# Linear attention and a gated MLP on one core: banks of two classic products, half the copies of m on VectorE, one of eight products by 1/den on Pool

## Chip, cores, metric

One core of one Trainium2 chip runs the whole kernel. The metric is the device time of one execution in microseconds. The kernel before took 230.46 us (median of three runs, 230.44 to 230.59). TensorE is written PE, VectorE DVE, ScalarE ACT and GpSimd POOL, as in the profile. The calls ran on different chips (1, 2, 1 and, for the last kernel, 15; that of the first result is not on record), so times are compared within a call and ratios between calls.

## The reference

2048 tokens, width 512, 32 heads of 16, gated width 896, all in bf16:

```python
def _A_ref(x, wqkv, wo):                       # linear attention
    q, k, v = ...                              # x @ wqkv, 32 heads
    phi = lambda t: jnp.where(t > 0, t + 1, jnp.exp(t)) + 1e-06
    pq, pk = phi(q), phi(k)
    kv = einsum('bhsd,bhse->bhde', pk, v);  z = einsum('bhsd->bhd', pk)
    num = einsum('bhqd,bhde->bhqe', pq, kv)
    den = einsum('bhqd,bhd->bhq', pq, z)[..., None] + 1e-06
    return heads_joined(num / den) @ wo
def _B_ref(x, w_in, w_sp, b_sp, w_out):        # gated MLP
    z = gelu(x @ w_in);  z1 = z[..., :Fh];  z2 = layernorm(z[..., Fh:])
    g = einsum('ts,bsf->btf', w_sp, z2) + b_sp[None, :, None]
    return (z1 * g) @ w_out
h  = x + _A_ref(layernorm(x), A_wqkv, A_wo)
h2 = h + _B_ref(layernorm(h), B_w_in, B_w_sp, B_b_sp, B_w_out)
```

## The kernel before

The program is a list of operations with their dependencies. A stored permutation, ORDER, gives the queue of every engine. An operation that is recorded through a helper carries the helper's line, so L402 is any product, L421 any ACT instruction and L555 any normalization. The parts that matter here (cuts marked with `# ...`):

```python
    for c in range(KD):                            # m = block-diagonal(kv) @ wo, KD = 4
        b = CB[1 - c % 2]
        matmuls(bank(b), [(kvm[:, c, :], wo[:, c, :])])
        act(m[:, c, :], bank(b), ACT.Copy, GW)     # four copies PSUM -> SBUF on ACT
    # ...
    for tg in range(NG):                           # four groups of 512 tokens
        # den on PE, 1/den by Ln and Exp on ACT, spread by 4 DMAs into r16, then
        for t in range(first, tg + 1):
            for c in range(0, KD, 2):
                q, r = pqT[:, c:c + 2, t * GW:(t + 1) * GW], r16[t // 2][:, c:c + 2, t % 2, :]
                dve(lambda v, q=q, r=r: v.tensor_tensor(q, q, r, ALU.mult), [q, r], [q], 2 * GW, acc=2)
    # ...
    for n in range(NT):                            # 16 tiles of 128 tokens
        b = AB[n % 3]
        matmuls(bank(b), [(pqT[:, c, n * P:(n + 1) * P], m[:, c, :]) for c in range(KD)])
        dve(... scalar_tensor_tensor(h[:, n, :], bank(b), 1.0, x[:, n, :], ..., accum_out=s[:, 0:1]) ...)
        act(sh_t[n % 2], h[:, n, :], ACT.Square, D, ...)
        # per pair of tiles: mean and variance in five small steps on POOL, the last of them
        pool(lambda p: p.tensor_tensor(r, ve, expo..., ALU.pow), ...)            # rs, L546
        # then, per tile of the pair:
        norm("DVE", hn, h[:, i, :], ...)           # DVE tensor_scalar bf16 -> bf16, L555
        dma_t(hnT[:, :, i * P:(i + 1) * P], hn, f"ht{i}")                         # transposing DMA
    # ...
    for q in (0, 1):                               # ungated half of z, most of it by Strassen
        for tg in (2 * q, 2 * q + 1):
            classic(KF - 1, tg, 6)                 # the odd block as plain products, in bank 6
        # ... strassen(k, q, ZB[...], ...): banks 4 to 7
```

Names used below: a bank is a part of PSUM, numbered 0 to 7, to which PE writes a product. m is the block-diagonal kv times wo; h is x plus the attention's output, hn its normalization and hnT the transpose of that, made by DMA. The products of hnT with the half of w_in that becomes z2 (L807 and L810, win2 in the prediction) make, for one tile of tokens, a gated unit. wsp holds w_sp transposed and, until that is loaded, the sums of blocks that Strassen's scheme needs, in which seven block products do the work of eight; a classic product is one done without the scheme.

## Time and profile before

| | before |
|---|---|
| time | 230.46 us |
| span of the profiled run | 229.2 us |
| PE busy | 221.9 us (97%), 1168 of 1191 matmuls in the trace |
| DVE / ACT / POOL busy | 76% / 48% / 21% |

PE is the bound. The page's busy shares, the table by stage and PE's waits stand in the prediction, with how to read them. Timeline columns are start, duration, engine, line, operation, what it writes and reads, and in brackets how long the engine was idle before it and who ended that.

A product by 1/den takes 0.69 us.

### The profile page before, as it was taken

The page shows a single profiled execution, that of the slowest core. Times are in us where ns is not written, and L with a number is a line of the kernel's source. Part 1 is how long each engine was busy: PE and PEld are TensorE (multiplying, and loading weights), DVE is VectorE, ACT ScalarE, POOL GpSimd, SP SyncE. Part 2 cuts the span into 40 slices and gives each one's busy share as a digit, 9 for nine tenths or more (in the row PEclk, how much of TensorE's full clock was granted, in tenths as well). Part 3 has the DMA queues.
Part 4 walks back from the last instruction along what each step waited for, and adds up shares of the span by engine and source line. Part 5 has one row for each costly group of instructions (what it writes and reads, how often), then busy time and mean ns, then how long its engine had stood idle before and what let it go on. Part 6 is the DMA issues. An engine that isn't in the chain of part 4 may idle for free.

```text
span 229.2 us, 3241 instructions
## 1 busy us (share of the span) xinstructions
PE 221.9 (97%) x1168; PEld 110.0 (48%) x1191; DVE 174.5 (76%) x347; ACT 109.6 (48%) x205; POOL 47.7 (21%) x134
## 2 busy tenths in 40 slices
PE   8899999999899999999999999999999999999995
PEld 7344444453344444444434444444455555555553
DVE  3999756937996979489988888678738688885295
ACT  5695943499889989999456102100022122021110
POOL 3444400000764584467600000000000000000000
PEclk9999999999999999999999999999999999999999
DMA  6942469928645149499900799800000000020025
GB/s 186 280 131 47 93 177 331 268 79 196 147 108 106 38 92 111 96 184 224 125 0 1 153 234 177 172 0 0 3 0 0 0 26 24 0 69 3 0 83 169
DMA packets 58896, 23.68 MB, mean 103 GB/s; under 512 B 48512, under 2 KB 58752, under 8 KB 58880
## 3 DMA queue, kind: packets, MB, share of 16 engines
q1 hardware_dynamic: 58176, 22.88, 44.8%
q10 hardware_dynamic: 704, 0.59, 0.8%
q8 instruction: 9, 0.15, 0.2%
q14 instruction: 7, 0.06, 0.1%
HBM read 7.47 MB, written 2.10 MB: 42 GB/s over the span
## 4 chain that ended last, share of the span: by engine, by line
PE 91%; DVE 2%; issue 2%; POOL 1%; DMA 1%; ACT 1%
PE psum L402 72%; PE psum L807 6%; PE psum L659 6%; PE psum L810 5%; DMA x<-in_A_x_dram 1%; ACT sh L421 1%; DVE h L981 1%; DVE h L781 1%; POOL rs L550 1%; ACT m L421 0%; PE psum L755 0%; POOL st L534 0%; PE psum L680 0%; PE psum L569 0%; PE psum L724 0%
## 5 line engine op out<-in xcount | busy, mean ns | idle before, releaser
L421 ACT ACTIVATE psum<-psum 128x256 f32<-128x256 f32 (+1 forms) x39 | 17.7, 467 | 83.6 <-PE psum L402 57.0
L402 PE MATMUL psum<-wsp,z 128*128 128x512 bf16 x200 | 47.6, 379 | 0.4
L402 PEld LDWEIGHTS psum<-wsp,z 128*128 128x128 bf16 x208 | 20.4, 98 | 22.5 <-ACT psum L421 0.2
L421 ACT ACTIVATE e<-psum 128x1024 bf16<-128x1024 f32 (+1 forms) x18 | 16.7, 927 | 12.7 <-PE psum L402 12.0
L402 PE MATMUL psum<-t,s 128*128 128x512 bf16 x96 | 22.5, 379 | 0.0
L421 ACT ACTIVATE z1T<-psum 128x512 bf16<-128x512 f32 x28 | 16.1, 601 | 8.1 <-PE psum L402 5.5
L402 PE MATMUL psum<-wsp 128*128 128x256 bf16 (+1 forms) x89 | 19.3, 315 | 0.4 <-DVE psum L856 0.4
L402 PE MATMUL psum<-wout,z1T 128*128 128x256 bf16 (+1 forms) x82 | 16.5, 314 | 0.1
L807 PE MATMUL psum<-win,hnT 128*128 128x512 bf16 x63 | 16.2, 379 | 0.1
L989 DVE TENSOR_TENSOR u<-psum,bsp 128x512 bf16<-128x512 f32 x16 | 11.0, 689 | 6.0 <-PE psum L402 5.9
L402 PE MATMUL psum<-xnT,wqkv 128*128 128x512 bf16 x61 | 15.2, 379 | 0.2
L659 PE MATMUL psum<-pk,xn 128*128 128x512 bf16 x64 | 15.3, 379 | 0.0
L421 ACT ACTIVATE z<-psum 128x896 bf16<-128x896 f32 x16 | 14.6, 913 | 1.3 <-PE psum L810 1.0
L402 PE MATMUL psum<-wqkv,xnT 128*128 128x512 bf16 x61 | 14.7, 379 | 0.2
L402 PE MATMUL psum<-m,pqT 128*128 128x512 bf16 x62 | 14.4, 379 | 0.3 <-DVE h L781 0.2
L989 DVE TENSOR_TENSOR u<-psum,p 128x512 bf16<-128x512 f32 x12 | 8.3, 688 | 8.1 <-PE psum L402 8.0
L402 PEld LDWEIGHTS psum<-t,s 128*128 128x128 bf16 x96 | 9.4, 98 | 10.0
L810 PE MATMUL psum<-win,hnT 128*128 128x384 bf16 x64 | 13.0, 326 | 0.0
L510 DVE BATCH_NORM_STATS2 st<-x 128x6 f32<-128x512 bf16 x15 | 9.7, 677 | 3.8 <-DMA x<-in_A_x_dram 3.8
L781 DVE SCALAR_TENSOR_TENSOR h<-psum,x 128x512 bf16<-128x512 f32 x16 | 10.8, 686 | 2.1 <-PE psum L402 2.1
L534 POOL TENSOR_SCALAR st<-st 128x1 f32<-128x1 f32 x10 | 3.9, 391 | 40.0 <-ACT sh L421 32.2
L402 PEld LDWEIGHTS psum<-wsp 128*128 128x128 bf16 x90 | 8.2, 98 | 8.2 <-DVE psum L856 1.0
(125 smaller groups left out, 382.4 us busy)
## 6 DMA issues: line engine op xcount, KB each, us to landing
r<-rcp SPq DMA_DIRECT2D x16, 128.0 KB, 2.7
out_dram<-h SPq DMA_DIRECT2D x15, 128.0 KB, 1.7
win<-in_B_w_in_dram SPq DMA_DIRECT2D x2, 896.0 KB, 5.5
x<-in_A_x_dram SPq DMA_DIRECT2D x6, 256.0 KB, 4.2
wqkv<-in_A_wqkv_dram SPq DMA_DIRECT2D x2, 512.0 KB, 5.8
wout<-in_B_w_out_dram SPq DMA_DIRECT2D x1, 896.0 KB, 7.3
wo<-in_A_wo_dram SPq DMA_DIRECT2D x1, 512.0 KB, 6.7
bsp<-in_B_b_sp_dram SPq DMA_DIRECT2D x1, 512.0 KB, 4.9
```

What stands on the lines that cost most here:

```text
L402: inst = pe.matmul(out_ap, lhsT=a, rhs=b, start=start and i == 0, stop=stop and i == len(pairs) - 1, **kw)
L421: return g.add("ACT", lambda ac: ac.activation(out_ap, in_ap, func, **kw), [in_ap, *extra], [out_ap] + ([accum] if accum is not None else []),
L510: dve(lambda v: v.bn_stats(s[:, 0:6], src[:, n, :]), [src[:, n, :]], [s[:, 0:6]], D)
L534: pool(lambda p: p.tensor_scalar(s[:, 2:3], s[:, 0:1], s[:, 0:1], -1.0 / (n * n), op0=ALU.mult, op1=ALU.mult), [s[:, 0:1]], [s[:, 2:3]], 240)
L550: pool(lambda p: p.tensor_tensor(r, ve, expo[:, 0:1], ALU.pow), [ve, expo], [r], 620)
L659: inst = pe.matmul(bank(CB[c]), lhsT=xn[:, i, c * P:(c + 1) * P], rhs=pk[:, i, :], start=i == 0, stop=i == NT - 1)
L781: dve(lambda v, n=n, b=b, s=s: v.scalar_tensor_tensor(h[:, n, :], bank(b), 1.0, x[:, n, :], op0=ALU.mult, op1=ALU.add, accum_out=s[:, 0:1] ...
L807: pe.matmul(bank(b), lhsT=hnT[:, c, n * P:(n + 1) * P], rhs=win2[:, c, 0:GW], start=c == 0, stop=c == KD - 1)
L810: inst = pe.matmul(bank(b + 1, F2), lhsT=hnT[:, c, n * P:(n + 1) * P], rhs=win2[:, c, GW:FH], start=c == 0, stop=c == KD - 1)
L981: dve(lambda v, o=o, q=q, add=add: v.tensor_tensor(o, q, add, ALU.add), [q, add], [o], DH2, ps=True)
L989: dve(lambda v: v.tensor_tensor(t, bank(b), add, ALU.add), [bank(b), add], [t], GW, ps=True)
```

## The change

The intent is to take work off the engine that was late at three places: two of the four copies of m go from ACT to DVE; one of the eight products by 1/den goes from DVE to POOL, which is 21% busy; the last two classic products (of token groups 2 and 3) leave bank 6, which the Strassen cells rotate through. The stored order was made anew for it.

```diff
-ORDER = "c-jrogMttU00qE@..."     (1011 entries, cut)
+ORDER = "c-jTQ17HvU00h8Cw..."     (the same 1011 operations, another order, cut)
@@ copies of m
-        act(m[:, c, :], bank(b), ACT.Copy, GW)
+        if c % 2:
+            dve(lambda v, c=c, b=b: v.tensor_copy(m[:, c, :], bank(b)), [bank(b)], [m[:, c, :]], GW, ps=True)
+        else:
+            act(m[:, c, :], bank(b), ACT.Copy, GW)
@@
-    DB, MERGE = 6, ()
+    DB, MERGE, PM = 6, (), ((3, 2),)
@@ products by 1/den
-                    dve(lambda v, q=q, r=r: v.tensor_tensor(q, q, r, ALU.mult), [q, r], [q], 2 * GW, acc=2)
+                    if (t, c) in PM:
+                        pool(lambda v, q=q, r=r: v.tensor_tensor(q, q, r, ALU.mult), [q, r], [q], 1800)
+                    else:
+                        dve(lambda v, q=q, r=r: v.tensor_tensor(q, q, r, ALU.mult), [q, r], [q], 2 * GW, acc=2)
@@ ungated half
+    last, _ = [next_pair() for i in (0, 1)], 0
-            classic(KF - 1, tg, 6)
+            classic(KF - 1, tg, last[tg - 2] if q else 6)
```

The lines shift: L768 of before is L774 after, L781 is L787, L807 is L813, L755 is L758.

More of the change, by code (lines that the diff above doesn't have):

```diff
@@ L15 @@
 SEM_NS = 45.0
-ORDER = "c-jrogMttU00qE@tj)G<d$VoZwz=81ZQHhO+jiZ}FHA&4MpVQ_03sm@q9HnBASPlVHsT;Y5+E1yAUE;?AdJumgRlsO;0S?m2#=5uk{}V1A{mk+1yUju5+fh-BNYmu5YnPNDxw0Kpb{D(9uguo(x4y;BONlJ2+|`EnUE1hQ4Cp88C8%OjnNcYP!-uw1KCj=-BAKv(F5I364j6c)zJ*i(Go4t6TQ#}z0n3WQ46h53bj!Obx|5+Fb3mL5A`t?<FO1&upDjC8aYuG<<K7O&>sWP7yZxy4bTvSFc3@85uI=t2XO?4FaZ-W8I!OAE3q0=Fb#vT4na7IV~BuNIDz9Bg5el}kywLK7>%izj?U<U8JLOrSb&o_jagWT^;nBDIE5E@iOG73DVnP1c!t@SgP|CP4cLf9Sd2~Bf$f-!dDx6C*o!^biGA3G-8hG{*otj9kNr4+E4YelxPaukh!jexRJx8ExP+Uyj9Yk%*LZ_hxQ#owi~G2T2MErG2*HqihX{Ox07m3{JjN4*W>|({DE`DJe83NU#AkfLH^kt-|GR(TJHFx%Vlo!PGaP>-G9xi6qi~wyG7e)i9#b(IQ!_L3Fh8>}I`c9O$*eRBFdqvtEz>bQGcY5?zX--mEXA^{$%M?t?99QOEX`a@z;cYwKo(+Q7GY7=VKLTXU6$YyCSqciXBpP!V%B2|wq^xZWF=N+71n11He@3<W^N{7awcVQCS!NDWG}8^8&+ixR%Z(KW;3Q_6Sm?~F5_CZWlwJ5R+eOHZDShs;ZP3a6pr9jj^uRC;Bby&HP&ELHfMTeP&>9~U+!UMrBzn#Wfo;uPMu*oWm5-sWIuLdS7uUwX4G~L;AoEFSPo<^1u?hssWS(09LIA9cXB4DaTaHDIp=UL=kYAh@jTaY0w?hT^XLe3sDJ{MSA~>cg;iWdRZvBAhwHh4CA5(jSxP0<jnmbIGc<$~IiLGjM!UG1`+0yzSxm=xmz7jnl~qnxc$}Mfj|+K_D|mt{d6I*<fQvYpr+A4oHA}NKM{|`-^E6)zv`~vwR^@e-Z&*QZSy4}TjaBrN&sbH}^oRHPjt^K}?^#0+d7Xb*Tc=r9{|G(j3*O)(zT{0d)nhi+WxnET-r{E7CiQ_e^@Yt<OJDhobrfFTxrz}KponUsAN<LW{Kfiepcbm9;0mFTil_K$rr$io!%U#n3?<3>#Lx<(u!^SWilKyxsYFVwBx<NeYOS_vshw)2U23CtilktQtoHiMSW2o+imfP$qi~9<xZ0?#I<L;^pdRX~ZtAED>aL#ZqCM)PUh1oU8mMjRuT8q7!RoC68ls^Zra>C6AdS)p?bB&J)M%a2SdGzmZP5;$)plLc1dY@<P0~88)_QH$8g0;8?bjn+)NUQrL><*$9nxhT&@mm?RUOuK9nn*r&~2U5HGS7f-O(vM(Oo^$3%%AGJr{gKFZDw=^;oZTPm8rgOSMePwL&YkN^kW}A9YK$d|warUVrsdAM{0E^+})gOW*Wce^kY^9L#n~|5H5&cL;ZIeTQ@?hjBQEc0&g^g2OtzQ#+EYx|$<9s-ro&J359_Ii{<-iPN~YV>_1PxRc{Mq2s!<<2i{FyM_}uk<&VzlRKHyJEJqWsq470Gdq(TIE$M(tFt?&v$>UPI*)U^ky|^5bGe`cozHEY--TSnh270{-POfh)XiPoJzUCVT*4*Y$E97?E!@)O+{JBO(cN9%ecjHL+|TXZ)6+f3z1-WAJ;hT!%`-gHgFVZ$-QNQ|$8$Zz^SsdWy};|e!Hd1fOT5ur9pvF2=*>Rv6CUAB9_lUL=3yS`?cV7Ze(6yj>m45Lah~Au9^;9g<Xzt5WnSUkUgNbs<&!?`Gd}BA-sipE@1?%z<v!r^KIhk7<&{3_BR=GVzTn5c<jcO|Cw}Uye&%bw;ak4r>%QsRe&`3j=evIEcYf~=PT>Ns?1;|mbx!IEj^Z~y=EHvO)qdpr{^<VzBaZh("
@@ new lines @@
+ORDER = "c-jTQ17HvU00h8Cwq47%ZQHhO+qGrewr$(CZ5wxy5Czc?4-pX=Q4t+65EHQw8*z{T0my|s$c?;6f}{WlBN&1s9Ks_6gwP0sWJrz_2!)hLgv7{){78kuNQ(lffJ$hJ%BYCOh>wIwjWj5NbSQ`nD2hTzk4z|rj3|z*$c!dvhAOCvEU1QTsEO<-fgb3FlIV%<D23{%f#zs|mS}}u=#9Pzi#}+L9H@mlsExX4i_&O=c8H657>6<_i~4AQ@fd@#Sb}9(j+`im@@S6^7=VH3hyLh@PUwuoID&&%iiT)}!5D-<jKl;?#AHlDNKC^Dti&p;#uN-e5Y}KQhT#y7;uwzO1R`KMrlJeFVkTx_6h>nmPGSM(V-`+hA=Y9&&fq0Z;RT-KDJJU~W@8S9V+1x}BNkyXHem<0V=m@lGqzw4_F^aYVHbAe9L{1Zw&6VX;{dMW3a;S-F5)_FAh|B#CNAR^-r^PB;5BX|h3?}H?&2OEAUNM41Vi#69w7qX;}bsPF`ghIBk==%;3vM}Bfj7l{@^QO68wj-48zb2#aJ|BGd#Z|9Dn04A~PDJG73{MH8V30^D_pcGYj)F4YQJr%Q%e3_)N=mOwSC=$O0_Qaumxj9}BW9voSk!FeeMKFpID#i!m5;u{;BqfVEhc37Ltxxr8lQoAp?dDOH@U*oLW;h>2N&Ygmz$SeaE=mA%=6ZCQ;q*pqd*m`hoo4cL&4*qBY&l+D?PYuTE;xQy+XoXJ><C76^+xQD5=g(+E+)!Bm0n1aJOf>W4Ad%2ZUnO@u2mm?X-AdccRPUj3RXM1*FM|NUo_TzSrW`FMB01o5|4&pv$P$p$m7iLvjW!4d9(M-<bY^GB-<y3Z^;Zf$$Ssr69bz^P~<zVL16?SEJUS$E@;a$$*7>?ymj^i$l=St4yD$e61F62E<;C;^L5Dw#HF5n_g(L_$wG)>nG&D1Q-)*Q{%Jk8evEmSfsQXb`3A>~zJ71SG+P%#zJ6TW3p71uRB<ug`RN$qDTmDV}FV_B`^0j}o;{$V+lQ599tUw&alh1XYBQh7ztH&$10h0uHc;|D(Ac^>Bp9^^?vA9;vPR71OYffpH3HC0usSx2Y%oTvGM*ZGOx`H(mGh(EZIpV?H+)Lganl9%|3H@S(oSWUH6Ptnyvb=6X>R9~&tPVp5|G1Oj>6j_JaL7kOAj~P<|y3EadP3kriDwLwAjoPY#x~Q8vs;9cElX|F;daJK`sjC_)w4|L%q*&^wsOql)imgEkqo4f6-;ATgiYqIuk|>(ODV~BUskUmD8f&12sE^KTm<DTvhHI!UXrx9dP@{EP54A^QG*;uaQQNdb+qFrTG(i(JPLs4wtF>O6bw+EnMQe3Y`?OnEv_V07r2RUmLwc-pI-tEetHZjiBRZ;Mdajo`uB&>g6S}68I;HEnttYypXL_L<TC62ns%2WP6<VoPx~tcEqnr9J_?7PIt={Q}Zt0`$>w(_ui$18fzv`QQ>!<$cpFZics+yLA`LFDhuI68=<N6Na;I82Y4(U)1<8Th`MvmwRuIXA%<**L#XpZj4j^Y@O=~%Arrf%lcuIna_<JfNKxK7}Nj_3GJ>?H2!PHyf1CvsY+b8;th7pHdyXLK58b|z<WYiD;(XLTOuc0G4?Hs^3I7jz-#cRm+(5f^m}H+CDhbxU`5D;IY$mvA?ic1f3YJNI-cmvK4wa(nl12X}R4S8#9lb$M5EAD?tT_xEHE@IX)X6c6@v&+vM0@DLC4OmFloPxB_v_GS<ANYC|FZ}A+@^9XPAcJJ^`@Ag8^_b%`8Vh4GF7kQ{h`M8IBw8uEmV?E9%Jl+#L(R;n$OTFCteA;Jxz^gpTD}BmGeb(oE-Uofehy219{n!`$(y#o)PkqUkeZ^OO-8X&Bw|&F6e8;c-%=diPOT5f0{J;<W*6;k@YrV!FoYW~?(NP`Ad0oJ(eavrM#fSae_x;H0{L%jbZ<+T*"
```

## The prediction

> **What bounds the kernel now.** I read the page's busy shares first, then the table by stage, then what TensorE (PE) waited for, then PE's timeline where it waits. The page:
> ```profile
> PE 221.9 (97%) x1168; PEld 110.0 (48%) x1191; DVE 174.5 (76%) x347; ACT 109.6 (48%) x205; POOL 47.7 (21%) x134
> PE 91%; DVE 2%; issue 2%; POOL 1%; DMA 1%; ACT 1%
> ```
> PE is busy 221.9 of 229.2 us and is 91% of the chain that ended last. [...] the run of 28 products with m below takes 6.21 us, 0.22 us each, at granted clock 1.00. [...] The table by stage (first column the stretch, then its length and PE's busy time) shows where it does not stream:
> ```profile
> 0.00:8.53 8.53, 6.34 (x67) 5.46 (x69) 4.22 (x11) 4.67 (x12) 3.79 (x22) 1.00 0.68 210
> 8.53:48.00 39.47, 39.23 (x199) 17.79 (x202) 32.15 (x64) 24.82 (x35) 8.88 (x23) 1.00 0.70 185
> 48.00:76.80 28.80, 27.67 (x147) 12.38 (x150) 21.66 (x53) 26.53 (x54) 10.23 (x25) 1.00 0.55 119
> 76.80:109.70 32.90, 32.74 (x164) 15.96 (x165) 26.92 (x57) 30.30 (x60) 21.54 (x58) 1.00 0.70 127
> 109.70:130.00 20.30, 19.83 (x91) 8.72 (x92) 18.19 (x27) 9.68 (x18) 3.23 (x7) 1.00 0.36 59
> ```
> Idle PE by difference: 2.19 in the head, 0.24, 1.13, 0.16, 0.47 us. After 130 us there is 0.53 us more, in crumbs of 0.05 us, and the tail of 2.7 us (last add, store). The waits between 8.5 and 226 us that have a name are few:
> ```profile
> PE psum L755 <- DVE pqT L584: 0.5, 1, 0.5
> PE psum L402 <- DVE psum L856: 0.4, 1, 0.4
> PE psum L402 <- DVE h L781: 0.2, 1, 0.2
> ```
> and two of them stand in the handover from attention to the gated block:
> ```profile
> 52.89 0.87 PE L402 MATMUL psum<-wo,kvm 128*128 128x512 bf16 x2
> ...
> 55.76 6.21 PE L402 MATMUL psum<-m,pqT 128*128 128x512 bf16 x28
> 62.52 0.40 PE L755 MATMUL psum<-pqT,zc 128*32 128x512 bf16 x4 [0.55 <-DVE pqT L584]
> 63.13 1.04 PE L402 MATMUL psum<-m,pqT 128*128 128x512 bf16 x4 [0.21 <-DVE h L781]
> 64.00 1.03 PE L807 MATMUL psum<-win,hnT 128*128 128x512 bf16 x4
> ```
> The pair of wo products takes 0.87 instead of 0.59 us: 0.28 us in which the last one waits for a copy of m to leave its bank. So all that any reordering can give back is 0.55 + 0.21 + 0.28 + 0.40 = 1.44 us, unless it shortens head or tail. That is 0.6% of 230.46.
>
> [...] the trace has 0.608 us for ScalarE's copy of m, and 0.69 us for VectorE's reads of 512 from PSUM. [...] the same Pool step on one element took 0.30 and 1.12 us.
>
> **The change part by part.** The number of matmuls stays the same. The order of all five queues is a stored permutation, and it is replaced as a whole; I walked the new queues by hand with durations of the trace.
>
> *Copies of m.* Removed from ScalarE: 2 x 0.61 = 1.2 us (about 0.5 us each at their pace). Added to VectorE: 2 x about 0.65 = 1.3 us, around 51 to 55 us, where VectorE had gaps of 2.6 and 1.4 us. So it is hidden. On the path: the first two wo products stand behind an unchanged run of PE work, and the third now waits for VectorE, which is free from 51.9 us. The fourth waits for ScalarE's copy, which follows the Ln/Exp of group 1 and ends at 53.4 us, while PE is there at 53.2. So about 0.25 us of the old 0.28 stays. The first product with m needs ScalarE's second copy (about 55.8) and VectorE's second product by 1/den (55.6); PE is ready at 55.8. Net 0.
>
> *The handover after it.* The new queue runs 32 products with m before the last denominator product (28 before). VectorE now does two 1/den products ahead of the second h, and hn0 ahead of the fourth h, so hn0 (waiting for Pool, about 60.9) holds up h. In my walk n=4 waits 0.15 us and n=6 waits 0.8 us for their banks, and the first win2 product starts at 64.15 instead of 64.00. So the old 0.55 + 0.21 is not removed; it comes back as roughly 0.9: +0.15 us.
>
> *The Pool product.* Removed from VectorE: one of eight, 0.69 us (0.6 at its pace), around 72 us. [...] The products that need it (tokens of group 3) come in the new order after one more win2 unit (1.51 us), at 74.7 us. The other half, still on VectorE, waits for its transfer until about 74.0 and is done at 74.75. [...] Statistics queued behind the Pool product have slack of more than one win2 unit. I take +0.05 us.
>
> *The banks of the last two classic products.* They leave bank 6, which the Strassen cells rotate through, for the pairs 0/1 and 2/3, free once the win2 products end. Nothing is computed less. What it gives is that two products of 0.86 us no longer stand in a queue for bank 6 with 16 gelus and copies, so they can fill the hole at 118 us (0.40 us, a VectorE add at L856). I credit 0.3.
>
> *The wsp transposes.* Five half-row transposes stood ahead of the last rows of hnT; in the new order two do, and 14 are issued behind. At 1.36 us each plus 0.58 for bsp from about 93.9 us the last is issued at 114 and lands some 4.8 us later, about 119. The first product that needs that group is at about 120.5 (14 win1 products, 3.0 us, now come before the first wsp product at 109.7; then 36 products more, 7.8 us). Thin, but hidden: 0, with risk upwards.
>
> *Tail.* The last add still waits for a 0.77 us group of products; 2 instead of 4 adds stand in front of it: -0.05 us.
>
> Sum: -0.03 + 0.15 + 0.05 - 0.3 - 0.05 = -0.2 us. I add -0.2 us for a judgement of mine: an order found by search is likelier to have closed more holes than a hand walk sees. 230.46 - 0.4 = 230.05; I say 230.0.
>
> **Rivals.** *The order closes all named holes:* 230.46 - 1.44 = 229.0. For: the pieces each remove work from the engine that was late. Against: hn0 ahead of h, seen in the new queue. *Pool becomes the bound at 74 us:* if the product takes 3.5 us [...], group 3 waits 1 us and the statistics behind slip too: 231 to 232. For: the 1.12 us Pool step; against: one instruction only, with PE work of 1.5 us put in front. *The transposes come too late:* if DMA delivers 14 half rows at 1.6 us instead of 1.36, 3 us at 120 us, of which 1.5 hidden: about 232. For: DMA share is near 1.00 around 100 to 110 us; against: before, ten of them and bsp were through by about 112 us. *VectorE becomes the bound:* +1.3 - 0.7 us over 76% busy; only the order matters, not the sum.
>
> **Range and chances.** The floor is 229.0, so faster by over 2% (below 225.9) would need a stage to lose matmuls, which none does: 0.01. Slower by over 2% (above 235.1) needs 4.6 us of new waits; two rivals together give about 3: 0.02. Range 229.2 to 231.2.
>
> **What would show it.** Right: PE's busy time stays within 0.5 us of 221.9; a PE wait of some tenths for VectorE's h near 60 to 62 us; [...] no PE wait for Pool; no wait at 118; no wait for the wsp transfers. Wrong: a PE wait over 1 us in any stage, a Pool product over 3 us, or a head other than 8.5 us.

Its sum, -0.03 + 0.15 + 0.05 - 0.3 - 0.05, came to -0.18, rounded to -0.2, and with the judgement of -0.2 to -0.4. The marks stand for passages on the hardware that no trace of this case shows. The largest of them is the duration of the POOL product, and with it the time at which it would end, the margin by which it would be hidden and its range among the signs. The trace before has POOL's tensor_tensor on one or two elements only, so the +0.05 us stands as a judgement of mine, not as a walk with durations of the trace; the 3.5 us of the rival and the 3 us among the signs are assumptions as well. The "about 0.65" us for a copy of m on DVE lies between the 0.69 us of DVE's reads of 128x512 from PSUM in that trace and the 0.61 us from start to start of two of them in a row (h at 58.91 and 59.52 us); in the trace after, the copies took 0.69 us each. To stream is meant as starting products without a gap.

## More of the kernel before

One more stretch will matter: the one around 72 us, where the products by 1/den of the last token group (L768) stand between normalizations (L555).

```profile
71.69 0.41 DVE L555 TENSOR_SCALAR hn<-h,st,rs 128x512 bf16<-128x512 bf16 x1 [0.58 <-POOL rs L546]
72.01 0.69 DVE L768 TENSOR_TENSOR pqT<-pqT,r 128x1024 bf16<-128x1024 bf16 x1
72.61 0.41 DVE L555 TENSOR_SCALAR hn<-h,st,rs 128x512 bf16<-128x512 bf16 x1
```

A normalization takes 0.41 us, 0.33 at its pace.

DVE had slack: its last product for this group ended at 72.70 us, and the 16 products that read it started on PE at 73.22 us without a wait.

## The result and the profile after

| | before | after |
|---|---|---|
| median, same rounds | 230.50 us (230.44 to 230.86, 6 runs) | 231.53 us (231.18 to 231.77, 6 runs) |
| ratio after to before | | 1.004 (95% interval 1.0027 to 1.0053) |
| span of the profiled run | 229.2 us | 229.8 us |

A ratio here is the mean time of one kernel's fast runs over that of the other's of the same rounds, so it is not quite the ratio of the medians quoted beside it. The kernel became slower by 1.0 us, where a gain of 0.4 us was predicted. By the limit of 2% it counts as the same, but it lies outside the predicted range.

The page of the kernel after, busy time and the chain by engine:

```profile
PE 224.1 (98%) x1191; PEld 111.3 (48%) x1191; DVE 175.9 (77%) x348; ACT 108.0 (47%) x203; POOL 50.1 (22%) x135
...
PE 88%; DVE 4%; DMA 3%; ACT 2%; POOL 1%; issue 1%; SPq 0%
```

PE's busy time is 2.2 us more than before. But this trace has 23 matmul records more (1191 against 1168), so that is no added work: the prediction's sign "within 0.5 us of 221.9" can't be read from these two traces. The chain has more DVE in it (4% against 2%). PE's waits after (engine, what it was about to write, line, releaser: total, times, longest; a wait of 1.0 us for the warm-up at the start, in both kernels, is left out):

```profile
PE psum L402 <- DVE pqT L774: 0.9, 1, 0.9
PE psum L569 <- DVE xn L555: 0.6, 1, 0.6
PE psum L813 <- DMA hnT<-hn: 0.2, 1, 0.2
```

The three old waits (L755, L402 for L856 and for L781) are gone from this list, as hoped. A wait of 0.9 us for a product by 1/den on DVE (L774) is new, as is one of 0.6 us in the head. The table by stage (stretch; its length and PE's busy time) of after:

```profile
8.53:48.00 39.47, 38.83 (x201) 17.52 (x200) 31.13 (x60) 23.91 (x33) 8.66 (x25) 1.00 0.67 175
48.00:76.80 28.80, 27.61 (x148) 11.81 (x147) 23.22 (x54) 25.62 (x50) 13.29 (x30) 1.00 0.48 106
76.80:109.70 32.90, 32.90 (x165) 15.91 (x164) 25.52 (x57) 29.46 (x60) 17.02 (x43) 1.00 0.57 108
109.70:130.00 20.30, 20.30 (x96) 8.98 (x94) 18.64 (x32) 10.84 (x21) 7.81 (x19) 1.00 0.93 163
```

From 76.8 to 130 us PE shows no gap at all, where before had 0.16 + 0.47 us (0.36 us of it the wait at 118 us; some of the rest may be records that before's trace lacks). The loss lies before that. The three timelines of after where it is largest, PE first:

```profile
74.06 0.81 PE L816 MATMUL psum<-win,hnT 128*128 128x384 bf16 x4
75.74 3.63 PE L402 MATMUL psum<-m,pqT 128*128 128x512 bf16 x16 [0.86 <-DVE pqT L774]
```

```profile
71.94 2.52 DVE L555 TENSOR_SCALAR hn<-h,st,rs 128x512 bf16<-128x512 bf16 x2 [0.22 <-POOL rs L546]
74.39 0.68 DVE L787 SCALAR_TENSOR_TENSOR h<-psum,x 128x512 bf16<-128x512 f32 x1
...
75.00 0.68 DVE L774 TENSOR_TENSOR pqT<-pqT,r 128x1024 bf16<-128x1024 bf16 x1
```

```profile
71.20 0.71 POOL L546 TENSOR_TENSOR rs<-st,expo 128x2 f32<-128x2 f32 x1
71.87 2.12 POOL L772 TENSOR_TENSOR pqT<-pqT,r 128x1024 bf16<-128x1024 bf16 x1
74.09 0.42 POOL L534 TENSOR_SCALAR st<-st 128x1 f32<-128x1 f32 x1
```

Here is the cause. The product on POOL took 2.12 us (71.87 to 73.99). What changed is beside it: DVE's two normalizations, started 0.07 us after it, took 2.52 us instead of 0.73. The group view of the two (least, median, longest in ns; first and last start) splits them:

```profile
L555 DVE TENSOR_SCALAR hn<-h,st,rs x2: 401/1300/2200, 71.9 to 74.1; 128x512 bf16<-128x512 bf16 x2
```

The first took 2.20 us and ended at 74.14, 0.15 us after POOL's product; the second 0.40. So the next h ended at 75.0 us, DVE's own half of the product at 75.7, and PE, ready at 74.88, started at 75.74. In the trace the held-off instruction looks busy: DVE has no idle time there. That is why a look at idle times finds nothing.

To place the rest, I read three stretches in every trace at the same work: to the first product with m; from there until the 64 products with m and the first four gated units are done; from there to the end of the span.

| kernel | to first m product | until the 64 are done | to the end |
|---|---|---|---|
| before | 55.76 | 22.42 | 151.02 |
| after | 56.29 | 22.91 | 150.60 |

After that work is done (78.18 us before, 79.20 us after) the kernel after gains 0.42 us. It loses 0.49 us in the middle and 0.53 us in the head.

### The profile page after: what moved, and what is told of

It is laid out like the page before. It is cut to its first block, busy times and chain, and to the rows that moved or that the text cites. A ratio compares the mean times of both kernels' runs of the same rounds, so it can differ in the third digit from the quotient of the medians.

```text
span 229.8 us, 3276 instructions
## 1 busy us (share of the span) xinstructions
PE 224.1 (98%) x1191; PEld 111.3 (48%) x1191; DVE 175.9 (77%) x348; ACT 108.0 (47%) x203; POOL 50.1 (22%) x135
## 4 chain that ended last, share of the span: by engine, by line
PE 88%; DVE 4%; DMA 3%; ACT 2%; POOL 1%; issue 1%; SPq 0%
PE psum L402 71%; PE psum L659 6%; PE psum L813 5%; PE psum L816 3%; DMA x<-in_A_x_dram 3%; DVE hn L555 1%; DVE st L510 1%; DVE h L988 1%; PE psum L758 1%; ACT L805 1%; ACT sh L421 1%; PE psum L724 0%; ACT z L421 0%; PE psum L680 0%; PE psum L689 0%
## 5 line engine op out<-in xcount | busy, mean ns | idle before, releaser
L402 PE MATMUL psum<-wsp,z 128*128 128x512 bf16 x208 | 48.2, 379 | 0.0
L402 PEld LDWEIGHTS psum<-wsp,z 128*128 128x128 bf16 x208 | 20.3, 98 | 23.1 <-ACT psum L421 0.2
L402 PE MATMUL psum<-t,s 128*128 128x512 bf16 x96 | 22.2, 379 | 0.0
L402 PE MATMUL psum<-wsp 128*128 128x256 bf16 (+1 forms) x90 | 19.5, 315 | 0.0
L813 PE MATMUL psum<-win,hnT 128*128 128x512 bf16 x64 | 16.4, 379 | 0.2 <-DMA hnT<-hn 0.2
L402 PE MATMUL psum<-wout,z1T 128*128 128x256 bf16 (+1 forms) x83 | 16.3, 315 | 0.0
L402 PE MATMUL psum<-m,pqT 128*128 128x512 bf16 x64 | 14.9, 380 | 0.9 <-DVE pqT L774 0.9
L402 PE MATMUL psum<-xnT,wqkv 128*128 128x512 bf16 x64 | 15.3, 379 | 0.0
L402 PE MATMUL psum<-wqkv,xnT 128*128 128x512 bf16 x64 | 15.0, 379 | 0.0
L402 PEld LDWEIGHTS psum<-t,s 128*128 128x128 bf16 x96 | 9.4, 98 | 9.8
L581 DVE TENSOR_SCALAR e<-e 128x1024 bf16<-128x1024 bf16 (+1 forms) x18 | 7.1, 393 | 7.8 <-ACT e L421 7.7
L787 DVE SCALAR_TENSOR_TENSOR h<-psum,x 128x512 bf16<-128x512 f32 x16 | 10.8, 686 | 2.7 <-PE psum L402 2.7
L997 DVE TENSOR_TENSOR z1T<-u,z1T 128x512 bf16<-128x512 bf16 x28 | 11.5, 419 | 0.4
L402 PEld LDWEIGHTS psum<-wsp 128*128 128x128 bf16 x90 | 8.6, 98 | 6.6 <-ACT psum L421 1.0
```

What stands on the lines that cost most here:

```text
L402: inst = pe.matmul(out_ap, lhsT=a, rhs=b, start=start and i == 0, stop=stop and i == len(pairs) - 1, **kw)
L581: dve(lambda v: v.tensor_scalar(e, e, 1.0, EPS_PHI, op0=ALU.min, op1=ALU.add), [e], [e], w * GW, acc=4)
L787: dve(lambda v, n=n, b=b, s=s: v.scalar_tensor_tensor(h[:, n, :], bank(b), 1.0, x[:, n, :], op0=ALU.mult, op1=ALU.add, accum_out=s[:, 0:1] ...
L813: pe.matmul(bank(b), lhsT=hnT[:, c, n * P:(n + 1) * P], rhs=win2[:, c, 0:GW], start=c == 0, stop=c == KD - 1)
L997: dve(lambda v: v.tensor_tensor(z, t, z, ALU.mult), [t, z], [z], GW, acc=2)
```

## Experiments

My theory: the product on POOL holds DVE's normalizations off, and this costs most of the loss. Rivals: the new order itself costs it (head, handover), or the copies or the banks do. All kernels below gave the reference's result. The edits keep the stored order unless it is said. First four, each against before in five rounds (before 230.77 us).

**1. The product back on DVE** (after, at its place in the same order):

```diff
-    DB, MERGE, PM = 6, (), ((3, 2),)
+    DB, MERGE, PM = 6, (), ()
```

> The changed kernel with its one Pool product put back on VectorE, at its place in the same order. Theory 1 (the Pool product keeps VectorE from its two hn conversions, and TensorE waits 0.86 us at 75.7 us for the multiply behind them): the two conversions take 0.75 us together again instead of 2.52, the wait at 75.7 us falls below 0.1 us, and the time goes from 231.5 to 230.6 to 230.9. Rival (the new order costs the time, in the head and in the handover; the Pool product is not to blame, and VectorE's multiply would be late without it too): the wait stays above 0.6 us, 231.3 to 231.7.

Measured: 230.03 us, ratio to before 0.9964 (0.9952 to 0.9976). DVE and POOL of this kernel:

```profile
71.22 0.73 DVE L555 TENSOR_SCALAR hn<-h,st,rs 128x512 bf16<-128x512 bf16 x2 [0.32 <-POOL rs L546]
71.87 0.68 DVE L787 SCALAR_TENSOR_TENSOR h<-psum,x 128x512 bf16<-128x512 f32 x1
...
72.48 1.29 DVE L774 TENSOR_TENSOR pqT<-pqT,r 128x1024 bf16<-128x1024 bf16 x2
```

```profile
72.69 1.13 POOL L534 TENSOR_SCALAR st<-st 128x1 f32<-128x1 f32 x1 [1.50 <-ACT sq L421]
```

The normalizations take 0.73 us again, DVE does both products by 73.77 us, and PE starts the 16 products at 73.89 us without a wait. The time fell by more than expected: this kernel beats before. POOL's line shows the reverse of the same thing: a step on one element, started while DVE's products (both inputs in SBUF) ran, took 1.13 us and ended just after them (73.82 against 73.77 us). The same step (L534) takes 0.26 us at its quickest. The step of 1.12 us that the prediction had noticed in before is of this kind: it ran from 60.82 to 61.94 us, and ended 0.08 us after two DVE instructions in a row.

**2. The POOL product in four pieces:**

```diff
-   pool(lambda v, q=q, r=r: v.tensor_tensor(q, q, r, ALU.mult), [q, r], [q], 1800)
+   def parts(v, q=q, r=r):
+       inst = None
+       for i in range(2):
+           for j in range(0, GW, GW // 2):
+               u = q[:, i, j:j + GW // 2]
+               inst = v.tensor_tensor(u, u, r[:, i, j:j + GW // 2], ALU.mult)
+       return inst
+   pool(parts, [q, r], [q], 1800)
```

> The Pool product cut into four instructions of 256 elements each, the rest as in the changed kernel. If Pool holds VectorE off only for the length of one instruction, VectorE's conversions get in between the pieces: each conversion takes at most 0.4 + 0.6 us, the two together under 2.0 us, the wait of TensorE falls to 0.3 us or less and the time to about 231.0. If it holds it off for every access [...], the pair stays at about 2.5 us and the time at 231.5, or a little more for the fixed cost of three more Pool instructions. Rival of the order: 231.5 with the pair's duration not mattering.

Measured: 230.54 us, ratio 0.9989 (0.9973 to 1.0005). The group views of the normalizations (L555) and the pieces (L777) in this stretch, with least, median and longest in ns:

```profile
L555 DVE TENSOR_SCALAR hn<-h,st,rs x2: 747/750/754, 71.3 to 71.9; 128x512 bf16<-128x512 bf16 x2
```

```profile
L777 POOL TENSOR_TENSOR pqT<-pqT,r x4: 662/690/715, 71.2 to 73.2; 128x256 bf16<-128x256 bf16 x4
```

Each normalization got in between two pieces and took 0.75 us. So POOL held DVE off for one piece at a time (0.66 to 0.72 us). The other way round it was longer: the POOL step of experiment 1, started at 72.69 us, took 1.13 us and let pass even the second of DVE's products, which started only at 73.08. PE's wait fell to 0.22 us, and the time is 0.5 us above that of experiment 1, with another 0.19 us of waiting for a transpose in it. The pieces together take 2.64 us instead of 2.12.

**3. The normalizations later.** In DVE's queue the two normalizations of 71.9 us go behind the next h and behind DVE's own half of the product (two entries of the order moved, with the transposes that depend on them):

```diff
 DVE:  h(tile 10)
-  hn(tile 6), hn(tile 7), h(tile 11), product by 1/den
+  h(tile 11), product by 1/den, hn(tile 6), hn(tile 7)
```

> The Pool product stays; on VectorE the two hn conversions are moved behind the h of the next unit and behind VectorE's own half of the product. The h (from PSUM and one bf16 input) and the product (two bf16 inputs) now fall into the time of the Pool product. Theory 1 in its narrow form [...]: the h runs at its usual 0.6 us, the product starts when its transfer lands (about 74.0, when Pool is done) and takes 0.69 us, TensorE's wait falls from 0.86 to under 0.2 us, time 230.7 to 231.0. In its wide form (every VectorE instruction that touches SBUF is held off): the h takes up to 2.1 us, the product ends at about the same 75.0 us or 0.3 earlier, time 231.2 to 231.5. Rival of the order: no change, or slower where the conversions are now late (a wait for hnT of some tenths).

Measured: 231.27 us, ratio 1.0023 (1.0010 to 1.0036).

```profile
71.34 0.69 DVE L787 SCALAR_TENSOR_TENSOR h<-psum,x 128x512 bf16<-128x512 f32 x1
...
72.57 1.48 DVE L774 TENSOR_TENSOR pqT<-pqT,r 128x1024 bf16<-128x1024 bf16 x1 [0.54 <-DMA r<-rcp]
73.97 0.72 DVE L555 TENSOR_SCALAR hn<-h,st,rs 128x512 bf16<-128x512 bf16 x2
```

```profile
71.38 2.13 POOL L772 TENSOR_TENSOR pqT<-pqT,r 128x1024 bf16<-128x1024 bf16 x1
```

```profile
PE psum L402 <- DVE wsp L883: 0.9, 1, 0.9
```

The narrow form of the theory, in which only some of DVE's instructions are held off and h is not one of them, holds: the h, with one input from PSUM and one from SBUF, took its usual 0.69 us right beside the POOL product (it had started 0.03 us earlier, but POOL's product took its usual 2.13 us as well, so neither waited for the other); the product with two SBUF inputs took 1.48 us and ended 0.5 us after POOL's. PE's wait at 75 us was gone. But no time was won: the late normalizations made their transposes late, and PE waited 0.86 us at 78.9 us for the Strassen sum made of them. The wait was turned into another, which I had named only as a rival's effect "of some tenths".

**4. The POOL product alone on before** (order of before, no other edit):

```diff
+                    if (t, c) in PM:   # PM = ((3, 2),)
+                        pool(lambda v, q=q, r=r: v.tensor_tensor(q, q, r, ALU.mult), [q, r], [q], 1800)
```

> The kernel before with this one edit alone: the product of the last group's second pair of chunks goes to Pool, in the order of before. Theory 1: some VectorE instruction beside the Pool product takes 1.5 to 2 us longer than in the kernel before, and the time rises from 230.5 by 0.5 to 1.2 us. Rival of the order: the product on Pool takes 2.1 us but is hidden, 230.4 to 230.7.

Measured: 231.31 us, ratio 1.0021 (1.0009 to 1.0033), so 0.54 us slower than before.

```profile
71.51 2.52 DVE L555 TENSOR_SCALAR hn<-h,st,rs 128x512 bf16<-128x512 bf16 x2 [0.58 <-POOL rs L546]
```

```profile
73.61 3.63 PE L402 MATMUL psum<-m,pqT 128*128 128x512 bf16 x16 [0.41 <-POOL pqT L772]
```

The pair takes 2.52 us here too. In this order PE waits 0.41 us, and for POOL itself. So the cost does not come from the new order. But it is not the same wait: here PE feels that POOL's product itself is late (73.56 us, where DVE had ended it at 72.70), not the hold on DVE.

Second four, five rounds, before 230.75 us. They were run on another chip.

**5. The kernel after once more**, unaltered.

> The changed kernel once more, unaltered, on the chip and in the rounds of the next three. In its first profile two things cost: a wait of 0.64 us at 12 us for x of the fifth token tile (its transfer landed at 8.2 us) and the wait of 0.86 us behind the Pool product. Without the Pool product the same order had a wait of only 0.2 us in the head. If the 0.64 us was a late transfer of that one execution or chip, it is 0.3 us or less here and the first products with the normalized tokens start before 12.0 us, and this kernel is 0.8 to 1.1 us slower than the one without the Pool product (230.8 to 231.2, ratio to before 1.000 to 1.002). If it belongs to this kernel, the wait of about 0.6 us is here again and the ratio is 1.003 to 1.005.

Measured: 231.26 us, ratio 1.0019 (1.0007 to 1.0031). Of the two branches the ratio fits the first (the time is 0.06 us above it) and the head's wait the second: for xn PE waited 1.2 us here, in three pieces. But in the other kernels with the same head order it was anything from 0.2 to 1.4 us (1.4 in experiment 9), so it is not a property of this kernel. PE also waited 0.62 us behind the product and 0.40 us for a transpose before that.

**6. The head in the order of before**, without the POOL product (the first 120 entries of the old order, then the rest as after).

> The order after, Pool product back on VectorE, and the first 120 entries of the stored order as in the kernel before (statistics of the fifth tile and its mean before the sixth tile's statistics; wq loaded earlier). If the new order of the head costs something, TensorE's wait of 0.2 us for xn is gone and the time falls by 0.2 to 0.4 us against the same without this edit (230.0 on the last chip), to 229.6 to 229.8. If the head of the two orders is worth the same, 229.9 to 230.2.

Measured: 230.55 us, ratio 0.9985 (0.9972 to 0.9998). The expected gain of 0.2 to 0.4 us is not there; against the two measurements of the same kernel with the new head (0.9964, 0.9975) it is if anything slower. The rival of the head falls.

**7. All copies of m on ACT**, without the POOL product:

```diff
-        if c % 2:
-            dve(... tensor_copy(m[:, c, :], bank(b)) ...)
-        else:
-            act(m[:, c, :], bank(b), ACT.Copy, GW)
+        act(m[:, c, :], bank(b), ACT.Copy, GW)
```

> The changed kernel without the Pool product and with all four copies of m on ScalarE again: only the banks and the order are left. The prediction gave the copies a net of 0, with 0.25 us of the old wait of the last wo product staying. If that holds, 230.0 to 230.2, and the pair of wo products takes 0.8 us again. If the copies on VectorE are what frees the handover (the 7.94 us from the first product with m to the first win2 product, 8.24 before), the time rises by 0.3 us or more, to 230.4 to 230.7: ScalarE's second copy then comes behind its Ln and Exp.

Measured: 233.21 us, ratio 1.0108 (1.0086 to 1.0129), far outside either expectation.

```profile
PE psum L402 <- ACT m L421: 3.0, 2, 2.4
```

At their places in the new order the copies stand between Ln, Exp and other reads of PSUM in ACT's queue. The last one ended at 59.1 us; PE waited 2.44 us for it and 0.52 us for an earlier one. This measures how much the order leans on the edit, not what the edit gains.

**8. All classic products in bank 6**, without the POOL product (order repaired where the bank forbids it):

```diff
-            classic(KF - 1, tg, last[tg - 2] if q else 6)
+            classic(KF - 1, tg, 6)
```

> The changed kernel without the Pool product and with all classic products of the ungated half in bank 6 as before; the stored order is repaired where the other bank forbids it (the first legal entry is taken). The prediction credited the banks with 0.3 us, the wait of 0.40 us at 118 us. If that is right the wait, or another of 0.3 us or more after 109 us, is there again and the time is 230.3 to 230.6. If the order and not the bank had closed it, 229.9 to 230.2.

Measured: 244.81 us, ratio 1.062 (1.0595 to 1.0644). PE waited 9.5 us between 105 and 127 us for banks and results of the Strassen cells, and the granted clock was 0.965 to 0.986. This is a failed experiment: with the repaired order it is another kernel, and it tells nothing about the gain.

Third four, five rounds, before 230.97 us, made to have both kernels in the same rounds and to try two parts on the order of before.

**9 and 10. After without and with the POOL product, side by side.**

> The changed kernel without its Pool product once more, beside the unaltered changed kernel on the same chip and in the same rounds; so far the two were measured on different chips (0.9964 of before, and 1.0019 and 1.0044). If the Pool product costs what TensorE waits behind it (0.62 and 0.86 us in two profiles), this kernel is 0.6 to 0.9 us faster than the next one. If the product costs more (its descendants are late as well), 1.0 to 1.7 us. The waits of the head are those of this order: between 0.2 and 1.2 us, by chip.

> The unaltered changed kernel, for the pair with the kernel before it in this list. 231.0 to 231.6; TensorE waits 0.6 to 0.9 us for the product at 75 us; VectorE's pair of conversions takes about 2.5 us; the head's wait for xn should be the same as in the kernel without the Pool product on this chip, within 0.3 us, as the two have the same order there.

Measured: 230.32 us without (ratio 0.9975, 0.9962 to 0.9989), 231.07 us with (1.0009, 0.9996 to 1.0022). PE at the 16 products that need the group, without and with:

```profile
74.87 3.62 PE L402 MATMUL psum<-m,pqT 128*128 128x512 bf16 x16
```

```profile
75.16 3.63 PE L402 MATMUL psum<-m,pqT 128*128 128x512 bf16 x16 [0.90 <-DVE pqT L774]
```

The POOL product costs 0.75 us by the medians of the same rounds (230.04 to 230.71 us without, 231.01 to 231.53 with: no overlap); PE's wait is 0.90 us. In the profiled execution without the POOL product PE had also waited 0.59 us for a transpose at 64.5 us, in the other not; the spread of the runs is too wide to tell 0.75 from 0.90.

**11. The copies of m alone on before:**

```diff
+        if c % 2:
+            dve(... tensor_copy(m[:, c, :], bank(b)) ...)
```

> The kernel before with half of the copies of m on VectorE and nothing else, in the order of before. The prediction: net about 0; at best the 0.28 us of the second pair of wo products is gained (230.3 to 230.7 where before is 230.75). In the changed order the copies on VectorE were worth 3 us of waits for ScalarE; if they have a value of their own, it shows here as well as a shorter pair of wo products (under 0.7 us instead of 0.87). If VectorE's copies stand in front of its products by 1/den and delay them, the first product with m comes later than in before and the time rises by 0.2 to 0.5 us.

Measured: 230.77 us, ratio 0.9996 (0.9983 to 1.001). Net zero, as the prediction had it; the pair of wo products took 0.93 us here (53.11 to 54.04 us), as PE now waited for DVE's copy.

**12. The banks alone on before** (repaired order). With the stored order and the kernel's dependencies the repair comes out as this: on PE one of the two products moves four places back, and its gelu on ACT; all else keeps its place.

```diff
-            classic(KF - 1, tg, 6)
+            classic(KF - 1, tg, last[tg - 2] if q else 6)
```

> The kernel before with the banks of the last two classic products alone (the stored order repaired where the other bank forbids it; the queue of TensorE keeps all but the places of these two products). The prediction's credit of 0.3 us: the wait of 0.40 us at 118 us for VectorE is gone, 230.3 to 230.6 where before is 230.75. If the order has to be made for it, the wait stays or is replaced by another: 230.7 to 231.1.

Measured: 232.32 us, ratio 1.0056 (1.0044 to 1.0069); the helper's lines are shifted, L420 is L402 and L880 is L856:

```profile
PE psum L420 <- ACT z L439: 1.0, 1, 1.0
...
PE psum L420 <- DVE psum L880: 0.4, 1, 0.4
```

The wait for the add is still there, 0.36 us at 119.95 us, so leaving bank 6 alone does not remove it. And there is a new wait of 1.01 us at 108.2 us: by the code, a classic product now needs a pair of banks that a gated unit used, and the gelu (ACT z) that reads that unit has to end first.

The last kernel, in five rounds of its own with before at 230.69 us, asks why DVE is the loser.

**13. POOL's product one place later**, behind the one-element step that waits for ACT (with the operations that depend on it):

```diff
 POOL:  rs
-  product by 1/den, scale of st
+  scale of st, product by 1/den
```

> The changed kernel with the Pool product moved one place back in Pool's queue, behind the one-element step that waits for ScalarE's square (about 73.2 us). So VectorE's two hn conversions (71.9 us) start before the Pool product. If the engine whose instruction started first keeps the other out: the two conversions take 0.75 us again although the Pool product is there; h takes 0.69; VectorE's own half of the product and the Pool product meet at 73.3 us, and whichever is second takes 0.6 to 2 us longer; the Pool product ends at 75.3 to 76.1 us and TensorE waits 0.4 to 1.2 us for it or for the other half: 230.9 to 231.5. If Pool had precedence whatever the order, VectorE's half would be held off to the end of the Pool product and the one-element step before it would take its usual 0.2 to 0.3 us even beside VectorE's product.

Measured: 231.57 us, ratio 1.0039 (1.0023 to 1.0055).

```profile
71.30 0.73 DVE L555 TENSOR_SCALAR hn<-h,st,rs 128x512 bf16<-128x512 bf16 x2
71.95 0.68 DVE L787 SCALAR_TENSOR_TENSOR h<-psum,x 128x512 bf16<-128x512 f32 x1
...
72.56 0.69 DVE L774 TENSOR_TENSOR pqT<-pqT,r 128x1024 bf16<-128x1024 bf16 x1
```

```profile
72.98 0.40 POOL L534 TENSOR_SCALAR st<-st 128x1 f32<-128x1 f32 x1 [1.72 <-ACT sq L421]
73.44 2.12 POOL L772 TENSOR_TENSOR pqT<-pqT,r 128x1024 bf16<-128x1024 bf16 x1
```

```profile
75.62 3.63 PE L402 MATMUL psum<-m,pqT 128*128 128x512 bf16 x16 [1.28 <-POOL pqT L772]
```

Now nothing of DVE's was held off: 0.73 us for the pair, 0.69 for its product. For the pair that proves little, as POOL ran nothing beside it. The test is POOL's one-element step: begun at 72.98 us beside DVE's product, it took 0.40 us and ended 0.13 us after that product. The two long products did not meet, unlike what I expected. With experiments 1 (1.13 us for POOL's step beside DVE's products) and 3 (1.48 us for DVE's product beside POOL's) this says that where one held the other off, it was the one under way that kept the other out; POOL had no precedence. It doesn't help, as POOL's product now ends at 75.56 us and PE waits 1.28 us for it.

## Why the prediction was wrong

**The step that failed** is the POOL product, with its "I take +0.05 us." The length that I had assumed for it was shown by no trace; it took 2.12 us, and "no PE wait for Pool" came true. But the prediction looked for trouble in a longer POOL product, with 3.5 us as its rival. The runs show the effect on DVE: +1.79 us on its normalizations (2.52 us for the pair, where the kernel without the POOL product took 0.73). This term is 0.75 us by time in the same rounds, not 0.05. The reason in two steps: rs on POOL (L546) releases the normalizations, and the product stands right behind rs in POOL's queue, so that it started first (71.87 against 71.94 us). Then DVE's own half of the product, which the prediction had ended by 74.75 us, ended at 75.68.

What the traces show of who is held off: beside the POOL product a normalization took 2.20 us (0.41 alone) and a product with two SBUF inputs 1.48 us (0.69 alone), while the h from PSUM took its usual 0.69 us; beside DVE's products POOL's step took 1.13 us (0.26 at its quickest), and 0.40 us in experiment 13. Why a normalization is held off and h is not, they do not show.

The terms of the prediction's sum against the runs:

| term | predicted | measured |
|---|---|---|
| copies of m | -0.03 | 0 (experiment 11, ratio 0.9996); in the new order the pair of wo products takes 0.80 us for 0.87 |
| handover | +0.15 | about -0.1: 8.24 us from the first m product to the first win2 product in before (8.24 and 8.25 in 4 and 11, which have its order); 7.94 to 8.48, mean 8.15, in eight profiles of the order after |
| POOL product | +0.05 | +0.75 |
| banks and tail | -0.35 | -0.47 by the means of the last column below; but not of the banks alone |
| transposes | 0 | 0, no wait for them in any profile |
| all but POOL, with -0.2 of judgement | -0.43 | -0.74 and -0.65 (experiments 1 and 9, medians against before) |

The prediction's own sum is -0.18 and its total 230.08; it rounded to -0.2 and 230.05, which changes nothing. Its idle PE "by difference" is in part the 23 records that before's trace lacks (after's trace, with all 1191, shows no idle PE from 130 to 226.5 us); its sum doesn't rest on that.

The handover is right in kind and wrong in size. No wait for h stands in after's list, but its 32 products with m show that some were there:

```profile
56.29 7.56 PE L402 MATMUL psum<-m,pqT 128*128 128x512 bf16 x32
```

The 28 of before took 6.21 us, so 32 at the same pace are 7.08 by estimate, and 0.48 us went in pieces too short for the list, after h's that ended at 59.85 and 61.79 us. Against that the old 0.55 and 0.21 us are gone.

The stretches of the earlier table, in the profiles of the two orders as stored (the other edits left out):

| kernel | to first m product | until the 64 are done | to the end |
|---|---|---|---|
| before's order: before, 4, 11 | 55.76, 55.58, 56.04 | 22.42, 23.01, 22.44 | 151.02, 151.01, 151.12 |
| after's, POOL product: after, 5, 10 | 56.29, 56.12, 55.70 | 22.91, 22.91, 22.92 | 150.60, 150.47, 150.58 |
| after's, none: 1, 9 | 55.57, 56.01 | 21.77, 22.31 | 150.66, 150.58 |

- The last column: every profile of the new order is 0.35 to 0.65 us shorter after the attention than every one of the old. The predicted closing of the hole at 118 us is near in size. Its reason is not shown: the banks alone left that wait in place and cost 1.35 us (experiment 12). In the new order with the new banks the wait is gone; whether an order alone could do it stays untested, as experiment 8 failed. That the size came out near is so in part luck.
- The middle column: with the POOL product 22.9 us to 0.02 in three profiles, without it 21.77 and 22.31. The difference of the latter two is the wait for a transpose (0.59 us in 9, none in 1). With the POOL product that wait does no harm (0.15, 0.40 and 0 us in the three, and the stretch is the same), since PE would wait for DVE later anyway. Waits in a row on the same engine are not to be added up.
- The first column scatters by 0.7 us within one order. The prediction's sign "a head other than 8.5 us" did come (7.83 us), but means nothing. Its other signs of being wrong did not: PE's longest wait, the warm-up's apart, was 0.86 us, and the POOL product took 2.12 us. No sign looked at the length of DVE's instructions.

**What stays open.** The POOL product's 0.75 us turns the predicted 230.0 into 230.7, and the new order without it was better than predicted. The time first measured, 231.53 us, is higher than the 231.26 and 231.07 us measured later for the same kernel, by ratio 1.004 against 1.0019 and 1.0009. By these later ratios it would be 230.7 to 230.9 us beside a before of 230.50, so 0.6 to 0.8 us has no shown cause. In its profile the head was late by 0.5 us, with a wait of 0.64 us for the fifth tile of x. That this head makes the difference in the other five runs too was not tested. Of the prediction's rivals the second fits best, "Pool becomes the bound at 74 us", 231 to 232: right in the size, wrong in its sign, a POOL product of 3.5 us (2.12 measured).

The version that beats both is the change without its POOL product: 230.03 and 230.32 us, ratios 0.9964 and 0.9975 to before, small but outside the noise in both.

## What to carry to other kernels

Before work goes from DVE to POOL, look at what DVE does in those same microseconds, and which of the two starts first: here a POOL product of 2.12 us held off a normalization (2.20 us instead of 0.41) and a product of two SBUF inputs (1.48 instead of 0.69) until it ended, while h, with one input from PSUM and one from SBUF, passed in 0.69. Look for durations that grew, not for idle time, since an engine that was held off was shown as busy here (all of the 2.20 us). And when an order was made for an edit, undoing the edit alone measures how the order leans on it; to find what the edit gains, try it on the old order as well.
